# Both Gram products of the first macro step in one group, its v scaled by VectorE, and second-layer residuals on VectorE

## The chip, the cores and the metric

The kernel runs on one core of a Trainium2 chip. The metric is the device time of one execution in microseconds, from start to end of the program on that core; the median of several runs counts. TensorE is the matmul engine (PE in the profile; PEld are its weight loads), VectorE is DVE, ScalarE is ACT, GpSimd is POOL, and SyncE (SP) issues the DMAs here. TensorE's clock has two levels, 1.2 and 2.4 GHz; the granted clock in the profile is the mean as a share of the full one.

## The reference

A delta-rule attention over 768 steps (4 batches, 8 heads, head size 48) gives 3072 tokens of 384 values, which go through two dense layers pairs:

```
for t in range(S):                                  # S = 768
    y[t]  = q[t] @ state
    v_old = kn[t] @ state                           # kn: k over its norm
    state = state + beta[t] * outer(kn[t], v[t] - v_old)
h   = x @ w_in                                      # 384 -> 1024
s   = h * softmax(h)
ln  = (s - mean(s)) / sqrt(var(s) + 1e-6) * g_ln
x2  = ln @ w_out                                    # 1024 -> 384
h2  = x2 @ w_in2                                    # 384 -> 2048
out = (h2 * sigmoid(1.702 * h2)) @ w_out2           # 2048 -> 384
```

The weights arrive as 64-bit floats.

## The kernel before

**Tiling.** The sequence is cut into 24 blocks of 32 steps; four blocks make a macro step, and there are six macro steps. For a macro step m the kernel computes for each of its blocks n the Gram products k.k and k.q (`gram(n)`), solves the triangular systems of all four blocks at once on VectorE (`solve(m)`, which writes the factors `dt` by way of DRAM), and then goes through the blocks in order (`recur(n)`): correction of v with the state, matrix of factors, output y, update of the state `mv`. `layer1(n, y)` does the first dense layer, softmax and normalisation of the block's 128 tokens and transposes the result; `layer1_out(g)` (tags B0 to B5) multiplies by `w_out` for 512 tokens, and `layer2(g)` (C0 to C5) does the second pair of layers for these. All large products are made of three fp16 products of high and low parts.

**Weights.** `weights()` converts 42 blocks: 6 of w1, 8 of wo1, 12 of w2 and 16 of wo2, in this order by layer, the last two mixed. A block is loaded (L476), turned from 64-bit to fp32 by ScalarE and VectorE (L479 to L491), rounded to fp16 on ScalarE (L504), and the rounding's residual becomes the low part. There are two ways for the residual. Up to block number `PRM["pe"]` (38.322) TensorE does it: an fp32 matmul with a scaled unit matrix (L510) and an fp16 matmul with a negative one (L511) leave the residual in PSUM, and ScalarE copies it out (L513). From there on (blocks 39 to 42) one VectorE instruction does it (L516).

**Gram products.** `gram(n)` loads k and q of the block (L560, L561), and `quads` issues 32 small fp32 matmuls (8 heads by 4 batches; the profile counts 64 for them, with as many weight loads) of a block into one PSUM bank. In the first macro step (m == 0) these are two groups: k.k with 32 columns (L577), and k.q with 32 columns (L594), with priority `late`. VectorE masks k.k (L586), writes it once more through another mask (L589, `below`), and masks k.q (L595). k.k is stored to DRAM (L597), and when all four blocks are there, the solve loads them (L606). In the later macro steps one group of 64 columns makes both.

**Scaling.** `recur(n)` multiplies v by a factor of `dt` on GpSimd (L736), before the first matmul of the block.

**Order.** Nothing in this kernel is ordered by hand. Every step is a task (`P.add`) with an engine, an assumed duration, what it reads and writes, and a priority. A planner (`Plan.emit`) goes through an assumed time and picks on each engine, among the tasks that could start first, the one with the lowest priority; the engines' programs are written in this order, DMAs in SP's. To a task's priority two tables add an offset: `OFF[tag]` and `OFF["tag|engine"]`, where the tag is that of the function's call (`gram0`, `w2_0_512`, `rec0`, `A0`, `B0`, ...). Where the planner sees TensorE pause before the first use of bank 0, it puts in filler matmuls on zeros (`busy`, recorded at L351).

Of the kernel before, what the change touches and what calls it, by code (L numbers as in the profile page):

```python
# [16 lines left out]
CH = 32  # L17
# [17 lines left out]
PRM = dict(bl=161.965, vm=-0.684, vo=-1.262, pe=38.322, near=22.976, al=0.0, af=0.658, xp=25.764, lp=1.945, go1=24.87, so1=49.904, ew=48, nx=6.743, kp=13.711, need=100.793, fg=0.161, f1=7.669, f3=1796.849, sp=0.084, gp=0.667, gq=99, cold=25.151, cf=-1.14, nb4=9.499, v1b=1.424, cut=0.473, el=22.0, la=0.602, d0=-55.31, d1=-18.518, d2=6.18, d3=1.2, a0=14.438, wo1s=1.606, nk=15.164, nb2=1.269, nb3=7.307, early=21.447, v1=-9.577, wa=0.829, U=36.161, T0=31.882, g0=0.697, a=-0.318, b=0.937, ao=18.661, go=231.282, gs=-2.989, so=-0.04, ss=0.661, w1=-840.745, wo1=-7.28, w2o=-52.255, w2s=8.446, wo2o=41.493, wo2s=4.056, nb=1.319, bs=0.333, cs=4.152, su=8.832, ld=47.69)  # L35
# [217 lines left out]
def kernel(  # L253
# [18 lines left out]
    PE, DVE, ACT, POOL, SP = nc.tensor, nc.vector, nc.scalar, nc.gpsimd, nc.sync  # L272
# [26 lines left out]
    w1 = [T("w1h", [128, K0, F1], FP16), T("w1l", [128, K0, F1], FP16)]  # L299
    wo1 = [T("wo1h", [128, K1, DM], FP16), T("wo1l", [128, K1, DM], FP16)]  # L300
# [44 lines left out]
    P = Plan()  # L345
# [7 lines left out]
    U, T0 = PRM["U"], PRM["T0"]  # L353
# [23 lines left out]
    def dve(n, f=1.0):  # L377
        return 0.145 + f * n / 960.0
# [4 lines left out]
    def pool(n):  # L383
        return 0.06 + n * 0.00207
# [155 lines left out]
    def quads(eng_fn, dur, r, w, prio, work=0.32):  # L540

        def mm():
            for h in range(H):
                for b in range(B):
                    eng_fn(h, b)
        P.add("PE", dur, mm, r=r, w=w, prio=prio, small=True, work=work)

    def gram(n):
        P.tag = f"gram{n}"
        m, s = divmod(n, SUB)  # L550
        base = due(SUB * m) - PRM["go1" if m == 1 else "go"] + PRM["gs"] * s if m else -1000.0 + s
        i, src = n % NKQ, kq[n]
        kb, lend = kqb[i], []
        if NKQ <= n < NKQ + 2:
            i, kb = f"l{n}", lnt[n - NKQ].bitcast(FP32).rearrange("p k t -> p (k t)")[:, 0:2 * H * 2 * CH].rearrange(
                "p (e h c) -> p e h c", e=2, h=H)
            lend = [f"lent{'hl'[n - NKQ]}{j}" for j in range(4)]

        def load():
            SP.dma_start(out=kb[64:64 + D], in_=src[0])  # L560
            SP.dma_start(out=kb[0:D], in_=src[1])  # L561
        P.add("SP", 2 * ISSUE, load, w=[f"kq{i}"] + lend, prio=base - 40, lat=2.2, nb=(0.0, max(base - 25, PRM["nb3"]), max(base - 25, PRM["nb4"]))[min(m, 2)])
        bk = Bank(SIDE)

        def product(c, w):
            def mm(h, b):
                r0, _ = cls(b)
                PE.matmul(bank(bk)[32 * b:32 * b + 32, 64 * h + c:64 * h + c + w], lhsT=kb[r0:r0 + D, b % 2, h, 0:CH],  # L568
                          rhs=kb[r0:r0 + D, b % 2, h, c:c + w], start=True, stop=True, tile_position=(r0, 32 * b))
            return mm  # L570
        gi = n % 2
        g_, p_, gp = gsb[gi], psb[gi], [f"gsb{gi}", f"psb{gi}"]
        if 2 <= n < 4:
            both = thb[n - 2].rearrange("p (a h c) -> p a h c", a=2, h=H)
            g_, p_, gp = both[:, 0], both[:, 1], [f"thg{n - 2}", f"th{n - 2}"]
        if m == 0:
            quads(product(0, CH), 0.6, [f"kq{i}"] + lend, [bk, gp[0]], base)  # L577
        else:
            quads(product(0, 2 * CH), 0.99, [f"kq{i}"] + lend, [bk] + gp, base, 0.37)
        mk = mask.unsqueeze(1).to_broadcast([128, H, 2 * CH])  # L580

        def ev(dst, c):
            return lambda: DVE.tensor_tensor(
                out=dst, in0=bank(bk).rearrange("p (h c) -> p h c", h=H)[:, :, c:c + CH],
                in1=mk[:, :, c:c + CH], op=ALU.mult)
        P.add("DVE", dve(256), ev(g_, 0), r=[bk, "mask"], w=[gp[0]], prio=base)  # L586
        late = base
        if m == 0:
            P.add("DVE", dve(256), lambda: DVE.tensor_tensor(  # L589
                out=below[s], in0=bank(bk).rearrange("p (h c) -> p h c", h=H)[:, :, 0:CH],  # L590
                in1=cross.unsqueeze(1).to_broadcast([128, H, CH]), op=ALU.mult),
                r=[bk, "cross"], w=[belowk[s], f"below{s}"], prio=base + PRM["bl"])
            late = -700.0 + n
            quads(product(CH, CH), 0.6, [f"kq{i}"] + lend, [bk, gp[1]], late)  # L594
        P.add("DVE", dve(256), ev(p_, CH), r=[bk, "mask"], w=[gp[1]], prio=late)  # L595
        gd = g_dr[m % 2][32 * s:32 * s + 32].rearrange("(h b) i j -> (b i) h j", b=B)
        P.add("SP", ISSUE, lambda: SP.dma_start(out=gd, in_=g_), r=[gp[0]], w=[f"gdr{m % 2}_{s}"],  # L597
              prio=base - 5, lat=dma(131072, 2))
        P.add("SP", ISSUE, lambda: SP.dma_start(out=p_dr[n % NPD], in_=p_), r=[gp[1]],
              w=[f"pdr{n % NPD}"], prio=late - 5, lat=dma(131072))  # L600
# [80 lines left out]
    def recur(n):  # L681
# [3 lines left out]
        m, s = divmod(n, SUB)  # L685
        base = due(n)
        md = m % 2
# [36 lines left out]
        def load_q():  # L724
            SP.dma_start(out=st[64:64 + D, 0:2], in_=qt[n, 0])
            SP.dma_start(out=st[0:D, 2:4], in_=qt[n, 1])
        P.add("SP", 2 * ISSUE, load_q, w=[f"stq{ist}"], prio=base - 20, lat=0.6, nb=base + 10 - PRM["ld"])

        def load_p():
            for b in range(B):  # L730
                w0 = cls(b)[1]
                SP.dma_start(out=st[w0:w0 + CH, b], in_=p_dr[n % NPD][32 * b:32 * b + 32])
        P.add("SP", 4 * ISSUE, load_p, r=[f"pdr{n % NPD}"], w=[f"stp{ist}"], prio=base - 20, lat=0.35, nb=base + 10 - PRM["ld"])

        dst, dk = (r_, f"r{ir}") if n == 0 else (v_, f"vt{iv}")
        P.add("POOL", pool(384), lambda: POOL.tensor_tensor(  # L736
            out=dst, in0=v_, in1=dt[:, s, :, CH:CH + 1].to_broadcast([128, H, D]), op=ALU.mult),
            r=[f"dt{md}_{s}", f"vt{iv}"], w=[dk], prio=base - 5)

        mvs = [f"mvs{c}" for c in range(4)]  # L740
        b1, b2, b3, b4 = Bank(SIDE), Bank(SIDE), Bank(SIDE), [Bank(SIDE), Bank(SIDE)]

        def hd(b):
            return bank(b)[:, 0:H * D].rearrange("p (h c) -> p h c", h=H)

        def ks(h, b):
            r0 = cls(b)[0]
            PE.matmul(hd(b1)[32 * b:32 * b + 32, h, :], lhsT=kr[r0:r0 + D, b % 2, h, :],
# [342 lines left out]
```

## Time and profile before

| | before |
|---|---|
| median of 3 runs | 839.51 us |
| runs | 835.08, 839.51, 845.69 us |
| profiled execution | 836.79 us |
| its span | 835.1 us |
| mean granted TensorE clock | 0.969 |
| TensorE, VectorE, ScalarE, GpSimd busy | 777.1, 589.5, 373.1, 247.2 us |

The span is from the first to the last instruction of the profiled execution; 1.7 us of its time lie outside. Durations below come from that execution. Busy time of TensorE contains fillers, and its records overlap, so the start of the next one is the better measure of what a matmul occupies.

### The profile page before, as it was taken

What the parts mean: (1) busy time and instruction counts of PE and PEld (TensorE: products, weight loads), DVE (VectorE), ACT (ScalarE), POOL (GpSimd) and SP (SyncE); (2) the same over time, 40 slices, a digit from 0 to 9 for tenths busy, and PEclk for the clock granted to TensorE, in tenths of its full rate; (3) what the DMA queues carried; (4) which work ended last, traced back from release to release, by engine and by line L of the source; (5) the groups of instructions that cost most, each with busy time, mean ns of one, the idle gap of its engine ahead of it and who ended that gap; (6) DMA issues with size and microseconds to landing.
All of it is one profiled execution on the core that took longest, in us unless ns stands there. A gap on an engine that the chain in (4) does not pass through costs nothing.

```text
span 835.1 us, 25208 instructions
## 1 busy us (share of the span) xinstructions
PE 777.1 (93%) x10642; PEld 389.7 (47%) x10642; DVE 589.5 (71%) x1456; ACT 373.1 (45%) x661; POOL 247.2 (30%) x240
## 2 busy tenths in 40 slices
PE   6568978999989999998999999999999999999997
PEld 4135554444555444544544444444444444444443
DVE  2896777999999999999999899964566445212111
ACT  0467564544326524544633545525554355422332
POOL 3020011110413354325531434504442222420322
PEclk7778898999999999999999999999999999999999
DMA  6898597976646466677736654365433252100101
GB/s 168 235 278 232 148 220 137 235 196 168 125 94 139 86 149 171 147 177 159 168 79 187 142 119 104 84 152 144 103 79 94 80 115 44 26 1 0 39 1 38
DMA packets 177314, 105.76 MB, mean 127 GB/s; under 512 B 128273, under 2 KB 161169, under 8 KB 177201
## 3 DMA queue, kind: packets, MB, share of 16 engines
q1 hardware_dynamic: 177200, 104.15, 52.7%
q8 instruction: 83, 1.36, 0.7%
q14 instruction: 31, 0.25, 0.1%
HBM read 66.16 MB, written 20.64 MB: 104 GB/s over the span
## 4 chain that ended last, share of the span: by engine, by line
PE 53%; DVE 27%; issue 9%; DMA 4%; ACT 3%; POOL 2%; POOLq 0%; SPq 0%; ACTq 0%; DVEq 0%
PE psum L1008 13%; PE psum L981 13%; PE psum L946 9%; PE psum L874 6%; DVE mv L836 4%; DVE trip L645 4%; DVE trt L642 4%; PE psum L568 3%; DVE th L989 2%; PE psum L351 2%; DVE mv L786 2%; DVE col L881 2%; PE psum L510 2%; ACT mv L782 2%; DVE eb L893 2%
## 5 line engine op out<-in xcount | busy, mean ns | idle before, releaser
L995 POOL TENSOR_TENSOR gl<-th,gh 128x512 f16<-128x512 f32 x90 | 107.3, 1192 | 236.0 <-ACT gh L992 167.8
L989 DVE SCALAR_TENSOR_TENSOR th<-th,psum 128x512 f32<-128x512 f32 x96 | 65.5, 683 | 89.0 <-ACT th L986 88.4
L1008 PE MATMUL psum<-gl,wo2h 128*128 128x512 f16 x288 | 109.1, 379 | 1.0 <-POOL gl L995 1.0
L1008 PE MATMUL psum<-gh,wo2h 128*128 128x512 f16 x288 | 109.5, 380 | 0.2 <-ACT gh L992 0.2
L981 PE MATMUL psum<-x2th,w2h 128*128 128x512 f16 x288 | 109.5, 380 | 0.1
L981 PE MATMUL psum<-x2th,w2l 128*128 128x512 f16 x288 | 109.1, 379 | 0.0
L981 PE MATMUL psum<-x2tl,w2h 128*128 128x512 f16 x288 | 109.1, 379 | 0.0
L1008 PE MATMUL psum<-gh,wo2l 128*128 128x512 f16 x288 | 109.1, 379 | 0.0
L986 ACT ACTIVATE th<-psum 128x512 f32<-128x512 f32 x96 | 56.9, 593 | 98.4 <-PE psum L981 93.6
L874 PE MATMUL psum<-w1h,xt 128*128 128x512 f16 x288 | 94.2, 382 | 1.5 <-DVE mv L836 0.8
L992 ACT ACTIVATE gh<-th 128x512 f16<-128x512 f32 x96 | 60.2, 627 | 68.9 <-DVE th L989 64.6
L1008 PEld LDWEIGHTS <-wo2h 128*128 128x128 f16 x576 | 56.2, 98 | 67.9 <-issue 2.1
L981 PEld LDWEIGHTS <-w2h 128*128 128x128 f16 x576 | 53.5, 98 | 62.0 <-issue 0.3
L642 DVE TENSOR_TENSOR trt<-trip 128x30 f32<-128x30 f32 (+9 forms) x150 | 71.3, 476 | 2.7
L645 DVE TENSOR_TENSOR trip<-trip,trt 128x30 f32<-128x30 f32 (+9 forms) x150 | 69.6, 464 | 2.4
L923 POOL TENSOR_TENSOR lnr<-eb,lnr 128x1024 f16<-128x1024 f32 x24 | 52.2, 2173 | 52.0 <-ACT lnr L921 52.0
L874 PEld LDWEIGHTS <-xt 128*128 128x128 f16 x432 | 40.0, 98 | 49.9 <-issue 2.5
L890 ACT ACTIVATE eb<-psum,col 128x512 f32<-128x512 f32 x48 | 36.9, 773 | 52.4 <-DVE col L886 52.1
L946 PE MATMUL psum<-lnth,wo1h 128*128 128x512 f16 x144 | 54.6, 379 | 0.4 <-DVE th L989 0.4
L874 PE MATMUL psum<-w1l,xt 128*128 128x512 f16 x144 | 54.8, 381 | 0.0
L946 PE MATMUL psum<-lnth,wo1l 128*128 128x512 f16 x144 | 54.6, 379 | 0.0
L946 PE MATMUL psum<-lntl,wo1h 128*128 128x512 f16 x144 | 54.6, 379 | 0.0
(210 smaller groups left out, 1246.6 us busy)
## 6 DMA issues: line engine op xcount, KB each, us to landing
kq<-kq SPq DMA_DIRECT2D x44, 192.0 KB, 4.4
stg<-w_in SPq DMA_DIRECT2D x11, 512.0 KB, 5.6
vt<-vt SPq DMA_DIRECT2D x24, 192.0 KB, 2.7
st<-qt SPq DMA_DIRECT2D x48, 96.0 KB, 2.9
kt<-kdr SPq DMA_DIRECT2D x48, 96.0 KB, 2.3
stg<-udr SPq DMA_DIRECT2D x48, 96.0 KB, 2.3
out<-ob SPq DMA_DIRECT2D x18, 256.0 KB, 2.7
ktr<-kd SPq DMA_DIRECT2D x46, 96.0 KB, 2.9
```

The lines of the kernel that those rows point to most:

```text
L642: DVE.tensor_tensor(out=tv, in0=tri[:, lo:hi, j:j + 1].to_broadcast([128, nr, j]), in1=tri[:, j:j + 1, 0:j].to_broadcast([128, nr, j]), op ...
L645: DVE.tensor_tensor(out=tri[:, lo:hi, 0:j], in0=tri[:, lo:hi, 0:j], in1=tv, op=ALU.add)
L874: PE.matmul(bank(bh[j]), lhsT=x[:, k], rhs=w_[:, k, 512 * j:512 * j + 512], start=(k == 0 and i == 0), stop=(k == K0 - 1 and i == 2))
L890: P.add("ACT", act(512) + 0.34, lambda j=j, ev=ev: ACT.activation(out=ev, in_=bank(bh[j]), func=ACTF.Exp, bias=cl(3), scale=cl(0), accum_o ...
L923: P.add("POOL", pool(F1), lambda: POOL.tensor_tensor(out=lnr[1], in0=e_, in1=lnr[0], op=ALU.subtract), r=["lnrh"] + [f"eb{ie}_{j}" for j i ...
L946: PE.matmul(bank(ba)[:, 0:w_], lhsT=wo1[a][:, k, oc], rhs=lnt[b][:, k, tk], start=(k == 0 and i == 0), stop=(k == K1 - 1 and i == 2))
L981: PE.matmul(bank(bh)[:, 0:w_], lhsT=w2[a][:, k, fc], rhs=x2t[b][:, k, tk], start=(k == 0 and j == 0), stop=(k == K0 - 1 and j == 2))
L986: P.add("ACT", act(w_), lambda: ACT.activation(out=th, in_=bank(bh)[:, 0:w_], func=ACTF.Tanh, scale=0.851 / (X2S * W2S)), r=[bh], w=[f"th{ ...
L989: P.add("DVE", dve(w_), lambda: DVE.scalar_tensor_tensor(out=th, in0=th, scalar=1.0, in1=bank(bh)[:, 0:w_], op0=ALU.add, op1=ALU.mult), r= ...
L992: P.add("ACT", act(w_), lambda: ACT.activation(out=gh, in_=th, func=ACTF.Copy), r=[f"th{i}"], w=[f"gh{i}"], prio=base)
L995: P.add("POOL", pool(w_), lambda: POOL.tensor_tensor(out=gl, in0=th, in1=gh, op=ALU.subtract), r=[f"th{i}", f"gh{i}"], w=[f"gl{i}"], prio= ...
L1008: PE.matmul(bank(acc[o])[:, 0:w_], lhsT=wo2[a][:, f, oc], rhs=gb[i][b][:, 0:w_], start=(f == 0 and j == 0), stop=(f == K2 - 1 and j == 2))
```

## The change

Three edits, and new tables.

- In the first macro step, too, one group of 64 columns makes both Gram products of a block. The separate group for k.q is gone.
- In the blocks of the first macro step v is scaled by VectorE instead of GpSimd.
- `PRM["pe"]` becomes 14: the 6 blocks of w1 and 8 of wo1 keep TensorE's way for the residual, and all blocks of w2 and wo2 take VectorE's.
- The table `OFF` has other numbers in all its entries, so the order on all queues can be another one. (Entries of engines that a task no longer uses are gone, as `w2_0_0|PE` and `rec0|POOL`.) No other parameter is changed.

```diff
-PRM = dict(bl=161.965, vm=-0.684, vo=-1.262, pe=38.322, near=22.976, ...)
+PRM = dict(bl=161.965, vm=-0.684, vo=-1.262, pe=14, near=22.976, ...)
...
-        if m == 0:
-            quads(product(0, CH), 0.6, [f"kq{i}"] + lend, [bk, gp[0]], base)
-        else:
-            quads(product(0, 2 * CH), 0.99, [f"kq{i}"] + lend, [bk] + gp, base, 0.37)
+        quads(product(0, 2 * CH), 0.99, [f"kq{i}"] + lend, [bk] + gp, base, 0.37)
...
             late = -700.0 + n
-            quads(product(CH, CH), 0.6, [f"kq{i}"] + lend, [bk, gp[1]], late)
         P.add("DVE", dve(256), ev(p_, CH), r=[bk, "mask"], w=[gp[1]], prio=late)
...
-        P.add("POOL", pool(384), lambda: POOL.tensor_tensor(
+        eng, cost, E_ = ("DVE", dve(384), DVE) if m == 0 else ("POOL", pool(384), POOL)
+        P.add(eng, cost, lambda: E_.tensor_tensor(
             out=dst, in0=v_, in1=dt[:, s, :, CH:CH + 1].to_broadcast([128, H, D]), op=ALU.mult),
-            r=[f"dt{md}_{s}", f"vt{iv}"], w=[dk], prio=base - 5)
+            r=[f"dt{md}_{s}", f"vt{iv}"], w=[dk], prio=base - 5, port=True)
```

## Rows read from the trace of the kernel before

**Rows 1.** The page, first part: busy time, share of the span, instructions.
```profile
PE 777.1 (93%) x10642; PEld 389.7 (47%) x10642; DVE 589.5 (71%) x1456; ACT 373.1 (45%) x661; POOL 247.2 (30%) x240
```

**Rows 2.** Busy time by stretch, all engines; then granted clock, DMA share, GB/s.
```profile
60.00:143.00 83.00, 69.31 (x1839) 43.21 (x1840) 59.22 (x142) 47.73 (x95) 10.33 (x8) 0.88 0.81 187
143.00:176.00 33.00, 31.96 (x508) 16.89 (x503) 30.04 (x95) 16.66 (x29) 5.52 (x4) 1.00 1.04 214
176.00:200.00 24.00, 24.00 (x226) 11.53 (x225) 23.59 (x66) 10.33 (x19) 0.00 (x0) 1.00 0.63 176
200.00:540.00 340.00, 327.35 (x4862) 164.89 (x4860) 317.92 (x779) 155.86 (x272) 133.90 (x120) 1.00 0.60 137
540.00:700.00 160.00, 158.53 (x2033) 77.06 (x2032) 92.85 (x219) 72.96 (x130) 51.07 (x48) 1.00 0.42 101
700.00:835.10 135.10, 129.17 (x597) 58.22 (x595) 26.10 (x48) 46.11 (x76) 37.05 (x31) 1.00 0.09 21
```

**Rows 3.** The chain that ended last, 6 to 26 us: start, us, what.
```profile
11.00 1.26 issue
...
15.31 2.32 issue
...
19.52 0.42 DVE th L583
19.94 0.34 DVE dt L589
...
20.69 2.87 issue
...
25.00 5.80 DMA trip<-gdr
```

**Rows 4.** DMA issues, 0 to 200 us: count, KB each, median us to landing.
```profile
gdr<-gsb SPq DMA_DIRECT2D x13, 128.0 KB, 4.0
...
lnth<-kq SPq DMA_DIRECT2D x2, 192.0 KB, 3.9
```

**Rows 5.** The timeline, SP and TensorE, first 160 us: start, us, engine, line.
```profile
9.08 0.43 SPq L561 DMA_DIRECT2D lnth<-kq  x1
...
13.00 1.08 PE L568 MATMUL psum<-kq 48*32 48x32 f32 x63
...
154.68 1.10 PE L568 MATMUL psum<-kq 48*32 48x64 f32 x64
```

**Rows 6.** Line 736 alone: ns shortest/median/longest, first and last start.
```profile
L736 POOL TENSOR_TENSOR vt<-vt,dt x23: 837/843/1286, 61.5 to 661.8; 128x384 f32<-128x384 f32 x23
...
L736 POOL TENSOR_TENSOR rb<-vt,dt x1: 3347/3347/3347, 58.2 to 58.2; 128x384 f32<-128x384 f32 x1
```

**Rows 7.** The chain that ended last, 0 to 200 us, further pieces.
```profile
58.22 3.36 POOL rb L736
...
66.12 0.94 PE psum L510 x2
...
131.56 0.22 PE psum L511
...
187.12 0.86 PE psum L510 x2
```

**Rows 8.** Groups by line and shape: busy us, mean ns of one, idle before.
```profile
L752 DVE TENSOR_TENSOR rb<-vt,psum 128x384 f32<-128x384 f32 x23 | 12.5, 545 | 6.6 <-PE psum L748 6.5
...
L483 DVE SCALAR_TENSOR_TENSOR fst<-fst,stg 128x512 int32<-128x512 int32 x7 | 4.8, 686 | 0.2
...
L483 DVE SCALAR_TENSOR_TENSOR fst<-fst,stg 128x384 int32<-128x384 int32 x6 | 3.3, 552 | 0.0
```

**Rows 9.** Line 511 alone, 60 to 143 us: ns, first and last start.
```profile
L511 PE MATMUL psum<-wo2h,neg x8: 326/326/326, 66.9 to 119.7; 128*128 128x384 f16 x8
L511 PE MATMUL psum<-w2h,neg x8: 379/379/634, 67.9 to 141.9; 128*128 128x512 f16 x8
```

**Rows 10.** Line 351 (fillers) by stretch: PE, PEld, granted clock, DMA share, GB/s.
```profile
143.00:176.00 33.00, 16.08 (x69) 6.43 (x69) 1.00 1.04 214
```

More of the change, by code (lines that the diff above doesn't have):

```diff
@@ new lines @@
+PRM = dict(bl=161.965, vm=-0.684, vo=-1.262, pe=14, near=22.976, al=0.0, af=0.658, xp=25.764, lp=1.945, go1=24.87, so1=49.904, ew=48, nx=6.743, kp=13.711, need=100.793, fg=0.161, f1=7.669, f3=1796.849, sp=0.084, gp=0.667, gq=99, cold=25.151, cf=-1.14, nb4=9.499, v1b=1.424, cut=0.473, el=22.0, la=0.602, d0=-55.31, d1=-18.518, d2=6.18, d3=1.2, a0=14.438, wo1s=1.606, nk=15.164, nb2=1.269, nb3=7.307, early=21.447, v1=-9.577, wa=0.829, U=36.161, T0=31.882, g0=0.697, a=-0.318, b=0.937, ao=18.661, go=231.282, gs=-2.989, so=-0.04, ss=0.661, w1=-840.745, wo1=-7.28, w2o=-52.255, w2s=8.446, wo2o=41.493, wo2s=4.056, nb=1.319, bs=0.333, cs=4.152, su=8.832, ld=47.69)
```

3 lines of the change are left out of this document (1 added, 2 removed).

## The prediction

> **What bounds the kernel now.** I first read the page's shares of busy time: TensorE is busy 93% of the span [rows 1], so the question is where its other 7% lies and how much of its work is not needed. The view of busy time in stretches answers that [rows 2]. From 200 us to the end TensorE idles 12.7, 1.5 and 5.9 us in three stretches that add up to 635 us: there the time is the matmuls themselves, and only fewer matmuls can shorten it. VectorE is at 94% from 200 to 540 us, but at 58% in the next stretch, so work added to it there is caught up long before the end. Up to 200 us the picture is another one. From 60 to 143 us TensorE idles 13.7 of 83 us at a mean granted clock of 0.88, and from 143 to 176 us it looks full only because 16.1 of its 33 us are filler matmuls on zeros [rows 10]. So the first 176 us, up to the first output product of layer 1, are a chain of waits (Gram products, solve, four recurrences, four softmaxes), and the change works nearly wholly in them. I then read the chain that ended last in that part, and priced each piece of the change from it.
>
> **Both Gram products in one group.** Today each of the four blocks' sequences of small matmuls stands twice, with 32 columns each, so that k.k leaves early and k.q follows. The chain shows what that costs. A second product starts only when VectorE has read the first out of the bank, twice (0.42 and 0.34 us), and part way through a second product TensorE stands still, three times, for 1.26, 2.32 and 2.87 us, waiting for nothing that the profile shows [rows 3]. The stops come at every second group of 64 matmuls, so I take them for something that counts instructions, their fetch; that is inferred. The last k.k leaves VectorE at some 20.3 us, and the load of all Gram blocks for the solve is issued at 25.00 us, after the last k.q product and its stop [rows 3]. In one group, half of the instructions go, and with them some two of the stops. What is late then is the last of the four input loads: its second half is issued at 9.08 us [rows 5] and lands 3.9 us after that [rows 4], at 13.0 us. A group of 64 columns takes 1.10 us later on, and one of 32 columns took 1.08 us here [rows 5], so I estimate 1.7 us. With one stop of 2.3 us and the eviction of 0.42 us the last block leaves at 17.4 us, its store lands 4.0 us later [rows 4], and the solve's load can be issued at 21.4 us: 3.6 us earlier. The bounds are 6 us (no stop at all) and 0 (the input loads move back on SP by as much, behind the weight loads that share its queue). A loss is excluded as long as SP's order puts these loads no later, since the group itself is shorter than the two that it replaces.
>
> The rows show a stop at every second group. The Trainium skill ("Runtime: NRT & Kernel Launch", Instruction fetch mechanics) says that crossing into the next block of instructions is "mostly hidden". By that rule no stop would go with the instructions, only the wait for VectorE ahead of the second products would, and the total would be 2 us worse; the trace, whose stops have no other releaser, speaks for the 3.6 us.
>
> **v scaled by VectorE.** The first scaling waits on GpSimd for the solve's factors and then takes 3.35 us, against a median of 0.84 us for the other 23 [rows 6]; it stands alone on the chain from 58.22 to 61.58 us [rows 7]. Why it is four times as long, no row tells. A VectorE operation of that size takes 0.55 us [rows 8], so 2.8 us go; the lower bound is 0.3 us (0.84 less 0.55), if this one was only unlucky. What is new is that the wait for the factors now stands in VectorE's queue: the weight conversions behind it wait too, and through them ScalarE's rounding. If the order puts it one conversion too early or too late, that is 0.55 to 0.69 us [rows 8]. The other three scalings add 1.6 us to VectorE, of which I count half, 0.8 us, as on the path; GpSimd had them free.
>
> **Second-layer residuals on VectorE.** 24 of the 38 weight blocks (twelve of w2, twelve of wo2) lose two fp32 passes, one fp16 matmul and one ScalarE copy each, and gain one VectorE operation. 16 of them lie from 60 to 143 us [rows 9], six from 143 to 176 us and two after that. The two after it lie in the TensorE-bound part and take 1.08 us each (0.86 [rows 7] and 0.22): 2.2 us go outright. The six lie among fillers, which take their place: nothing. Of the 16, seven stand on the chain, in 14 pieces from 66.12 to 131.78 us that add up to 9.4 us [rows 7]; the others lie beside it. In return VectorE gets one operation of 0.55 us for a block of 384 columns and of 0.69 us for one of 512, the price of its conversions of these shapes [rows 8]: 16 times 0.62 is 9.9 us in that stretch. VectorE is 71% busy there [rows 2], so part of it falls into its pauses and part delays the chain, which itself runs over VectorE in places. I take half, 5.0 us: net 4.4 us gained. The ends are 9.4 us gained (all hidden) and 0.5 us lost (none hidden).
>
> **The order.** Every task's offset is new, on all queues; which instruction then stands before which can't be read from the diff. After 200 us an order can gain at most the idle time that is left, 20 us [rows 2], most of which are short waits, and it can lose as much. I take zero, and 6 us either way in the range.
>
> **The sum.** 3.6, and 2.8 less 0.8, and 4.4 and 2.2 us make 12.2 us. The profiled execution took 836.79 us, so it would take 824.6 us. The median of the three runs before is 839.51 us, 2.7 us above it; the median counts, so the forecast is 827 us, 1.5% faster. A measurement of this kernel can tell about 2% from no change (its own runs spread over 1.3%), so the likeliest outcome is "within 2%".
>
> **The rivals.**
> First, more is gained. The 16.1 us of fillers before the first output product of layer 1 are waiting time of the fourth softmax and its transposes [rows 10]. If the new order lets that chain run with less between its steps, half of them go (8 us), and all of the 9.4 us with them (5 us more than counted): 814 us. For it: TensorE has room there. Against it: VectorE is 91% busy from 143 to 176 us and the DMA engines have none at all (share 1.04) [rows 2]. Chance 0.22.
>
> Second, the chain gives it back. An earlier start of the solve meets the same weight loads and conversions, and the recurrences wait for DMA and not for TensorE; then only the 2.2 us of the TensorE-bound part remain: 837 us. For it: the DMA share is 0.81 and 1.04 in the two stretches [rows 2]. Chance 0.21.
>
> Third, slower: VectorE becomes the bound of the first 176 us. It gets 22 residuals at 0.62 us and four scalings at 0.55 us there, 15.8 us. If all of that is on the path, and the saved TensorE time is only pauses, the head grows by 15.8 us and 2.2 us come back after it: 853 us. The point at which it decides is VectorE's busy share from 60 to 143 us: 59.2 us of 83 now [rows 2], about 71 of 83 after, which is 86% and not yet full. It would have to pass some 95%. Chance 0.07.
>
> Fourth, the clock. With some 15 us less of matmuls from 60 to 143 us (16 blocks at 1.08 us or three quarters of it), TensorE's granted clock there may fall from its mean of 0.88 [rows 2], between the two levels of 1.2 and 2.4 GHz, to some 0.7. The work that remains, about 52 us, would take 13 us more, half of it on the path: 834 us. Against it: the kernel puts in fillers where its plan sees a pause, and the clock stays at 1.00 where they run [rows 2, 10]. Chance 0.05. The Trainium skill ("TensorE: Matmul & The Clock Gate", Part 1) puts it as "the default state is throttled, and activity releases the throttle", which speaks against taking work off TensorE; the two stretches, at 0.88 with pauses and at 1.00 without, agree.
>
> That the change doesn't do what it says is hardly possible for the three edits, whose instructions are fixed by the code.
>
> **How the numbers follow.** The forecast's case has 0.45. Its own terms move it by some 8 us either way (the Gram groups between 0 and 6, the residuals between 9.4 and -0.5, the order by 6). The range reaches from 808 us, below the first rival, to 846 us, above the second and fourth, and leaves the third and the tails out. Faster by over 2% means under 822.7 us: a fifth of the forecast's case and nearly all of the first rival, 0.30. Slower by over 2% means above 856.3 us: the upper part of the third rival, 0.04. The rest, 0.66, is within 2%.
>
> **What would show it.** The load of the Gram blocks is issued near 21 us and no longer at 25 us, with one or two stops of TensorE before it. The first scaling is a VectorE operation near 0.55 us, and the first recurrence starts some 6 us earlier than at 61.6 us. TensorE has 14 residual blocks, none of them of the second layer. The first output product of layer 1 starts near 166 us instead of 176 us; from there to the end it takes as long as now less 2 us. I am wrong if that start is where it was with VectorE busy above 95% before it (third rival), if it is there with VectorE's pauses as now (second), or if the part behind it has changed by more than 6 us, which would be the order.

## The result and the profile after

The changed kernel takes 851.77 us, the kernel before 839.52 us, medians of 20 runs each. The ratio is 1.0144 with a 95% interval from 1.0119 to 1.0169: 12 us slower, where 12 us faster was predicted. It is within 2% of before, as the prediction held likeliest, but on the other side of the forecast and above its range (808 to 846 us). Two of the changed kernel's 20 runs took 909.75 and 1128.85 us at a lower granted clock, and the ratio leaves them out.

The profiled execution took 852.37 us (span 850.7, mean granted clock 0.967). Its page's first part, and its stretches (start and end; length; busy time of TensorE, its weight loads, VectorE, ScalarE, GpSimd, each with its count; granted clock, DMA share, GB/s), to hold against [rows 1, 2]:

```profile
PE 787.4 (93%) x10437; PEld 390.0 (46%) x10437; DVE 596.0 (70%) x1484; ACT 362.9 (43%) x637; POOL 245.1 (29%) x236
```
```profile
60.00:143.00 83.00, 69.33 (x1749) 42.45 (x1749) 55.13 (x148) 32.59 (x61) 5.94 (x4) 0.88 0.75 172
143.00:176.00 33.00, 31.55 (x380) 15.83 (x379) 31.31 (x92) 16.60 (x29) 7.64 (x4) 1.00 0.64 163
176.00:200.00 24.00, 22.60 (x224) 10.86 (x223) 21.64 (x55) 8.23 (x16) 1.35 (x1) 1.00 0.47 127
200.00:540.00 340.00, 322.27 (x4788) 161.96 (x4787) 311.35 (x763) 153.05 (x268) 128.89 (x115) 0.99 0.59 141
```

TensorE has 205 matmul records fewer and is busy 10 us longer, because it has 123 fillers more. VectorE, which got 24 residuals and four scalings, is busy 4.1 us less from 60 to 143 us than before, not 12 more: part of its work there comes later. The next rows are single lines of the same trace: SyncE's timeline (start, us) and TensorE's in the last Gram group, then groups by line with shortest/median/longest ns, first and last start: the first scaling, the fillers, and the output products of layer 1.

```profile
21.95 0.33 SPq L602 DMA_DIRECT2D trip<-gdr  x1
```
```profile
10.96 0.41 PE L568 MATMUL psum<-kq 48*32 48x64 f32 x10 [0.53 <-DMA kq<-kq]
12.53 1.05 PE L568 MATMUL psum<-kq 48*32 48x64 f32 x50 [1.16 <-issue]
```
```profile
L733 DVE TENSOR_TENSOR rb<-vt,dt x1: 537/537/537, 55.2 to 55.2; 128x384 f32<-128x384 f32 x1
```
```profile
L351 PE MATMUL psum<-zeros x251: 377/379/634, 1.1 to 178.5; 128*128 128x512 f16 x126
```
```profile
L943 PE MATMUL psum<-lnth,wo1h x144: 376/379/390, 178.7 to 778.6; 128*128 128x512 f16 x144
```

The first steps came as predicted. The solve's load is issued at 21.95 us (25.00 before [rows 3]), one stop of TensorE is left before it (1.16 us; one or two were predicted), the first scaling takes 0.54 us on VectorE (3.35 [rows 6]), and the first recurrence starts at 55.7 us instead of 61.6. Then the lead is lost: block 2's recurrence starts at 110.0 us (103.8 before), the first output product at 178.7 (175.9), and from there to the end it takes 672.0 us instead of 659.2. There are 251 fillers instead of 128. The granted clock doesn't tell the two kernels apart: 0.967 and 0.969 over the whole span.

### The profile page after: what moved, and what is told of

Its sections match the earlier page's. It is cut to its first block, busy times and chain, and to the rows that moved or that the text cites. A ratio compares the mean times of both kernels' runs of the same rounds, so it can differ in the third digit from the quotient of the medians.

```text
span 850.7 us, 24783 instructions
## 1 busy us (share of the span) xinstructions
PE 787.4 (93%) x10437; PEld 390.0 (46%) x10437; DVE 596.0 (70%) x1484; ACT 362.9 (43%) x637; POOL 245.1 (29%) x236
## 4 chain that ended last, share of the span: by engine, by line
PE 39%; DVE 31%; issue 3%; ACT 2%; DMA 2%; SPq 1%; POOL 1%; POOLq 0%; ACTq 0%; DVEq 0%
PE psum L978 13%; PE psum L1005 12%; PE psum L943 6%; PE psum L871 5%; DVE mv L833 4%; DVE trt L638 4%; DVE trip L641 3%; DVE th L986 2%; DVE mv L783 2%; DVE col L878 1%; DVE eb L890 1%; ACT mv L779 1%; PE psum L789 1%; DVE trip L629 1%; DVE rb L749 1%
## 5 line engine op out<-in xcount | busy, mean ns | idle before, releaser
L978 PEld LDWEIGHTS <-w2h 128*128 128x128 f16 x576 | 53.6, 98 | 62.3
L351 PE MATMUL psum<-zeros 128*128 128x512 f16 x251 | 66.1, 414 | 6.5 <-DVE zeros L350 6.5
L638 DVE TENSOR_TENSOR trt<-trip 128x30 f32<-128x30 f32 (+9 forms) x150 | 69.2, 461 | 2.2
L641 DVE TENSOR_TENSOR trip<-trip,trt 128x30 f32<-128x30 f32 (+9 forms) x150 | 67.3, 448 | 2.4
L920 POOL TENSOR_TENSOR lnr<-eb,lnr 128x1024 f16<-128x1024 f32 x24 | 55.7, 2320 | 41.4 <-ACT lnr L918 39.2
L908 POOL TENSOR_TENSOR col<-col,half 128x1 f32<-128x1 f32 x24 | 13.8, 575 | 175.4 <-DVE col L906 162.0
L943 PE MATMUL psum<-lntl,wo1h 128*128 128x512 f16 x144 | 54.6, 379 | 1.4 <-DMA lntl<-lnr 1.4
L871 PE MATMUL psum<-w1l,xt 128*128 128x512 f16 x144 | 55.1, 383 | 0.0
```

The source lines that it names most:

```text
L351: P.fill.append((gate, until, lambda: PE.matmul(psum[0], lhsT=z, rhs=z.unsqueeze(1).to_broadcast([128, 4, 128]), start=True, stop=True)))
L638: DVE.tensor_tensor(out=tv, in0=tri[:, lo:hi, j:j + 1].to_broadcast([128, nr, j]), in1=tri[:, j:j + 1, 0:j].to_broadcast([128, nr, j]), op ...
L641: DVE.tensor_tensor(out=tri[:, lo:hi, 0:j], in0=tri[:, lo:hi, 0:j], in1=tv, op=ALU.add)
L871: PE.matmul(bank(bh[j]), lhsT=x[:, k], rhs=w_[:, k, 512 * j:512 * j + 512], start=(k == 0 and i == 0), stop=(k == K0 - 1 and i == 2))
L920: P.add("POOL", pool(F1), lambda: POOL.tensor_tensor(out=lnr[1], in0=e_, in1=lnr[0], op=ALU.subtract), r=["lnrh"] + [f"eb{ie}_{j}" for j i ...
L943: PE.matmul(bank(ba)[:, 0:w_], lhsT=wo1[a][:, k, oc], rhs=lnt[b][:, k, tk], start=(k == 0 and i == 0), stop=(k == K1 - 1 and i == 2))
```

## The experiments

Three groups of runs. Medians are of 5 to 12 runs each beside the kernel before on the same chip (839.81 to 841.24 us); ratios are to it, with 95% intervals. A ratio isn't the quotient of the two medians and lies up to 0.2% from it (f_all, f_v), so small differences between runs are read from the ratios. The last four columns are each run's one profile, which can lie some us from its run's median (before 2.7 us under it, f_both 4.4 us above): granted clock from 60 to 143 us, and the start (us) of block 0's and block 2's recurrence and of the first output product.

| run | us | ratio | clock | rec 0 | rec 2 | output |
|---|---|---|---|---|---|---|
| before | 839.52 | 1 | 0.88 | 61.6 | 103.8 | 175.9 |
| changed | 851.77 | 1.0144 [1.0119, 1.0169] | 0.88 | 55.7 | 110.0 | 178.7 |
| f_gram | 834.0 | 0.9927 [0.9891, 0.9964] | 0.98 | 57.7 | 97.6 | 167.0 |
| f_v | 839.36 | 1.0014 [0.998, 1.0048] | 0.89 | 59.6 | 101.1 | 174.1 |
| f_gv | 838.43 | 0.9956 [0.9922, 0.999] | 0.94 | 54.5 | 98.1 | 169.1 |
| f_res | 841.18 | 1.0025 [0.9997, 1.0052] | 0.77 | 62.6 | 105.4 | 171.6 |
| f_both | 841.59 | 1.0007 [0.9974, 1.0039] | 0.90 | 62.1 | 106.4 | 176.6 |
| f_none | 840.03 | 0.9974 [0.9947, 1.0001] | 0.71 | 62.3 | 104.5 | 173.1 |
| f_all | 836.73 | 0.9983 [0.9951, 1.0016] | 0.75 | 53.2 | 98.6 | 165.8 |
| a_q | 851.46 | 1.0107 [1.0065, 1.0148] | 0.88 | 54.6 | 109.0 | 174.1 |
| f_hm | 843.47 | 1.0038 [1.0008, 1.0067] | 0.78 | 54.4 | 104.2 | 168.9 |
| h_fa | 842.73 | 1.001 [0.9978, 1.0043] | 0.71 | 55.6 | 101.1 | 170.5 |
| h_a2 | 852.52 | 1.0145 [1.01, 1.0189] | 0.84 | 55.2 | 114.3 | 179.7 |
| h_f2 | 857.76 | 1.0204 [1.0177, 1.0231] | 0.76 | 54.2 | 114.8 | 180.5 |
| h_w | 872.39 | 1.0382 [1.0346, 1.0418] | 0.85 | 62.8 | 114.2 | 196.7 |
| h_w2 | 872.33 | 1.0391 [1.0357, 1.0425] | 0.80 | 54.1 | 110.8 | 192.7 |
| r_off | 864.09 | 1.0274 [1.0228, 1.0321] | 0.94 | 61.3 | 109.9 | 194.2 |
| r_offb | 851.53 | 1.0141 [1.0108, 1.0174] | 0.79 | 52.9 | 94.1 | 181.8 |
| r_pert | 854.51 | 1.0163 [1.0123, 1.0202] | 0.94 | 63.2 | 105.2 | 172.9 |
| r_gram | 837.17 | 0.9957 [0.9923, 0.9991] | 0.84 | 57.2 | 99.0 | 172.1 |

### The edits, in the order of before

Here the planner goes on seeing the tasks of before, with their engines and durations; only what a task emits is another instruction. So the order is held, and an edit is seen without a new plan. Two theories stood at the start: the new order cost the time (1), or the work added to VectorE's queue did (2).

**f_gram**: one Gram group, at the first group's place.
```diff
-            quads(product(0, CH), 0.6, [f"kq{i}"] + lend, [bk, gp[0]], base)
+            quads(product(0, 2 * CH), 0.6, [f"kq{i}"] + lend, [bk, gp[0]], base)
...
-            quads(product(CH, CH), 0.6, [f"kq{i}"] + lend, [bk, gp[1]], late)
+            quads(lambda h, b: None, 0.6, [f"kq{i}"] + lend, [bk, gp[1]], late)
```


> The kernel before with the first edit alone: one group of 64 columns per block of the first macro step makes both Gram products, at the place of the first group; every other instruction of every engine stays where it was in the order of before. Theory 1 (the new order on the queues cost the time, the three edits themselves gain): the solve's load leaves SP near 22 us instead of 25, the recurrence starts some 3 us earlier, and 3 us or a little less reach the end: 836 us beside 839.5. Theory 2 (the edits that load VectorE's queue cost the time): says the same of this kernel, since VectorE gets nothing here. Were it slower than before, the group itself would be at fault.

It gained 0.73%, 6 us. Its chain up to the solve (start, us, what), against [rows 3]:
```profile
13.76 1.11 PE psum L568 x60
14.87 0.02 issue
14.89 0.42 DVE th L583
15.32 0.03 DVE dt L589
15.35 7.14 DMA gdr<-th
22.49 0.02 issue
...
22.55 4.85 DMA trip<-gdr
```
The stops of 1.3 to 2.9 us are gone, all of them; in their place the last store takes 7.14 us (4.0 was the median before [rows 4]). The load is issued at 22.55 us, 2.5 us earlier than before.

Where the stops stand tells more than their number. Counted with the fillers, the three of before come ahead of TensorE's 224th, 352nd and 480th matmul, 128 apart; the one in the changed kernel comes ahead of the 224th, with 64 columns instead of 32. In f_gram TensorE had waited for the input load nine matmuls ahead of that place, and there is no stop:
```profile
13.00 0.30 PE L568 MATMUL psum<-lnth 48*32 48x64 f32 x4 [1.76 <-DMA lnth<-kq]
```
So a stop goes with a count of instructions, and f_gram's missing one may only be covered by that wait.

**f_v**: `POOL.tensor_tensor(...)` becomes `(DVE if m == 0 else POOL).tensor_tensor(...)`, at the same place. **f_gv**: f_gram and f_v together.

> The kernel before with the second edit alone: the four scalings of v in the first macro step run on VectorE, each at the place in the order where GpSimd's stood; no other instruction moves. Theory 1 (order): the first takes 0.55 us instead of 3.35, so 2 to 3 us are gained: 837 us beside 839.5. Theory 2 (VectorE's queue): the scalings wait in VectorE's queue for the solve's factors and for the loads of v, the weight conversions behind them wait as well, and the time comes out at 842 to 846 us.

> The two edits of the first macro step alone, one Gram group and the scaling of v on VectorE, in the order of before; the residuals stay on TensorE. Alone the first gave 0.73%, the second nothing. If the two lie one behind the other on the chain into the first recurrence, as predicted, that starts near 54 us and the time is 831 to 834 us; if the second only moves a wait, 834 to 836 us.

The scaling alone moved the first recurrence by 2.0 us and the end by nothing that can be measured. With the Gram group it starts 3 us earlier than with that alone, and the end is no earlier: 838.43 us, above both ranges expected of f_gv. Theory 2's loss isn't there either.

**f_res**: VectorE's residual where ScalarE's copy stood, for the blocks after the 14th; TensorE's two products are left out.
```diff
-            P.add("ACT", act(n), lambda: ACT.activation(out=dl, in_=bank(bk)[:, 0:n], func=ACTF.Copy),
-                  r=[bk], ...
+            P.add("ACT", act(n), (lambda: DVE.scalar_tensor_tensor(out=dl, in0=fv, scalar=sc, in1=dh,
+                  op0=ALU.mult, op1=ALU.subtract)) if late else lambda: ACT.activation(...),
+                  r=[bk] + (fk + [wk + "h"] if late else []), ...
```
**f_both**: the same, but TensorE's products stay, unread. **f_none**: TensorE's products are left out and VectorE gets nothing; ScalarE's copy stays as `ACT.activation(out=dl, in_=fv, func=ACTF.Copy, scale=0.0)`.

> The kernel before with the third edit alone: the residuals of the 24 second-layer weight blocks that TensorE made are made by VectorE, each at the place in the order where ScalarE's copy stood; TensorE's passes for them are left out and not replaced. Theory 1 (order): 4.4 us in the first 176 us and 2.2 us behind it are gained, 833 us beside 839.5. Theory 2 (VectorE's queue): 15 us more work on VectorE before 176 us delay the recurrences and softmaxes, 845 to 850 us.

> As the third edit alone (residuals of 24 second-layer blocks on VectorE, 841.2 us), but TensorE's passes for these blocks stay in as well, with nobody reading their result. That run lost 1.7 us against before though TensorE had some 24 us less to do, and its granted clock from 60 to 143 us was 0.77 against 0.88. Theory A (TensorE's passes stood in pauses and held the clock up, so leaving them out gains nothing): here the clock is back at 0.88 or above, the matmuls of the four recurrences are as short as in before, and the time is 841 us or less. Theory B (leaving them out gained the predicted 6 us, and VectorE's added operations cost 8): here only the cost is left, 846 to 849 us.

> TensorE's passes for the residuals of the 24 second-layer blocks are left out, and VectorE gets nothing in their place: ScalarE's copy stays and writes zeros as the low part, so the second layer is computed without the low parts of these weights. This is the gain of taking work off TensorE by itself. Theory A (pauses and clock): at most 2 to 3 us, 836 to 840 us, with a granted clock below 0.88 from 60 to 143 us. Theory B: the predicted 6.6 us or more, 831 to 833 us.

The stretch from 60 to 143 us, one row each of f_gram, f_res, f_both and f_none (columns as above):
```profile
60.00:143.00 83.00, 70.11 (x1936) 42.35 (x1931) 65.13 (x173) 50.58 (x99) 8.02 (x7) 0.98 0.83 193
```
```profile
60.00:143.00 83.00, 59.52 (x1832) 40.96 (x1836) 69.01 (x160) 42.33 (x82) 11.34 (x8) 0.77 0.82 189
```
```profile
60.00:143.00 83.00, 68.72 (x1844) 42.59 (x1846) 66.11 (x158) 41.28 (x79) 10.98 (x8) 0.90 0.84 187
```
```profile
60.00:143.00 83.00, 63.40 (x1772) 42.85 (x1774) 61.07 (x143) 47.87 (x94) 11.14 (x8) 0.71 0.82 188
```
And the recurrence's products of the same step (ns, first and last start), of before and of f_none:
```profile
L765 PE MATMUL psum<-rb,dt x256: 198/248/284, 61.6 to 128.5; 32*32 32x48 f32 x128
```
```profile
L765 PE MATMUL psum<-rb,dt x256: 201/276/283, 62.3 to 129.1; 32*32 32x48 f32 x128
```
Without TensorE's passes the granted clock falls, from 0.88 before [rows 2] to 0.71, and the recurrence's own matmuls get longer, from a median of 248 to one of 276 ns. That isn't one profile's chance: over the whole span the clock is 0.947 to 0.959 in the twelve executions of f_none and 0.961 or more in 28 of the 29 of before beside them (0.957 in the other). f_none, which only takes work away, gains 0.26% (2.2 us, interval from 4.5 us gained to nothing). Theory A held; how much of the missing gain is the clock and how much the pauses in which the passes stood, these runs don't separate. f_res itself lies between the numbers of theories 1 and 2. With the passes kept (f_both), VectorE's operations cost 0.6 us, interval 2.2 us gained to 3.3 us lost; without them (f_res against f_none) 0.51%, 4.3 us, though the two intervals just touch. One place where f_res pays is the chain to the second layer; its view of TensorE's waits from 171 to 200 us:
```profile
PE psum L981 <- DVE x2tl L953: 3.7, 1, 3.7
```
The first product of layer 2 waits 3.7 us for an eviction that stands in VectorE's queue behind the second layer's weights.

**f_all**: the three edits at once. 

> The kernel before with all three edits, in the order of before: nothing but the changed instructions is in another place. It differs from the changed kernel in its order alone. Theory 1 (order): the predicted gain of about 12 us, or most of it, shows here: 827 to 833 us. Theory 2 (VectorE's queue): as slow as the changed kernel, 848 to 854 us.

836.73 us, between the two theories' numbers and much nearer to the first: theory 2 fell, and so did the predicted gain. The first output product starts at 165.8 us, where the prediction put it (166), but nine of these ten us are given back behind it (668.3 us to the end of its span, 834.1, instead of 659.2). TensorE is busy there for 639.2 us, as before (639.1), so the nine us are waits, 3.6 of them the wait for the second layer's first product that f_res has too. VectorE's busy time from 60 to 143 us is 70.9 us, as predicted (71), at a clock of 0.75:
```profile
60.00:143.00 83.00, 59.91 (x1762) 39.81 (x1753) 70.87 (x179) 40.18 (x76) 5.66 (x4) 0.75 0.76 180
```
f_all differs from the changed kernel in its order and in what the planner makes with it, the fillers (128 against 251) and the choice of PSUM banks. So **the order, with these, costs 1.0144 less 0.9983, 1.6% or some 13 us (15 by the medians), and the edits are worth 0.2% (interval 0.5% gained to 0.2% lost)**.

The two traces also tell where. Behind the first output product TensorE idles 29.0 us in the changed kernel and 29.1 in f_all; the changed kernel's 3.7 us more there are TensorE's work (643.0 us against 639.2). What the order costs is lost ahead of that product.

### The order, piece by piece

These runs have the changed kernel's tasks. The planner's result is collected, rearranged, and then emitted, in all of them but a_q with the PSUM banks given out anew:
```diff
-            t.fn()
+            self.out.append(t)
...
+    for i in ORDER:
+        tasks[i].fn()
```
"Old" is f_all's order, "new" the changed kernel's own. VectorE's waits from the first recurrence to the first output product (what waited, for what: us, times, longest), of the changed kernel and of f_all:
```profile
DVE col L853 <- PE psum L789: 6.5, 2, 3.3
DVE rb L773 <- PE psum L767: 5.2, 3, 3.7
DVE rb L749 <- PE psum L745: 3.8, 2, 3.6
DVE mv L783 <- ACT mv L779: 3.1, 4, 1.9
DVE wo2h L481 <- DMA wo2h<-w_out: 2.8, 1, 2.8
```
```profile
DVE mv L786 <- PE psum L757: 3.4, 2, 2.2
DVE rb L776 <- PE psum L770: 2.5, 2, 2.1
DVE wo2l L481 <- DMA wo2l<-w_out: 2.0, 1, 2.0
```
All such rows add up to 27.7 us in the new order and 12.1 us in the old. An instruction of VectorE's queue that waits holds up those behind it, and in the new order such waits are 15.6 us longer. The sum alone doesn't rank orders, though: from the same places of their traces it is 23.8 us in before and 23.1 in r_gram, which lose nothing.

**a_q** repairs the plainest place, by moving three tasks ahead of others: block 2's load of v (470) ahead of its loads of k, its scaling (473) and subtraction (475) ahead of a weight conversion. In the changed kernel block 2's subtraction (`rb`, L749) stood behind a weight load and its own v. On VectorE (start, us):
```profile
105.90 0.37 DVE L481 TENSOR_SCALAR wo2h<-wo2h 128x384 int32<-128x384 int32 x1 [2.81 <-DMA wo2h<-w_out]
...
107.90 0.56 DVE L733 TENSOR_TENSOR vt<-vt,dt 128x384 f32<-128x384 f32 x1 [0.57 <-DMA vt<-vt]
...
109.44 0.55 DVE L749 TENSOR_TENSOR rb<-vt,psum 128x384 f32<-128x384 f32 x1
```
```diff
+MOVES = [(470, 469), (473, 166), (475, 166)]
```


> The changed kernel in its own order, with three instructions moved: block 2's load of v goes on SyncE's queue ahead of the four loads of k for that block (93 us instead of 103.8), and its scaling and the subtraction behind it go in VectorE's queue ahead of the weight conversions whose loads are late (after the mask of gram 7 instead of after the wait at 105.9 us). Theory 1 (order; in the new order block 2's recurrence waits behind loads that others wait for in VectorE's queue): the first matmul of block 2's recurrence at 102 us instead of 110.0, and most of these 8 us reach the end: 844 to 846 us instead of 851.8. If the chain of the head is bound elsewhere, 850 us or more, with block 3 as late as now.

The subtraction now ran at 100.63 us, and yet block 2's recurrence started at 109.0. TensorE and VectorE in a_q:
```profile
100.63 0.55 DVE L749 TENSOR_TENSOR rb<-vt,psum 128x384 f32<-128x384 f32 x1 [1.69 <-PE psum L745]
```
```profile
102.66 0.38 PE L871 MATMUL psum<-w1h,xt 128*128 128x512 f16 x1
...
107.35 1.67 PE L351 MATMUL psum<-zeros 128*128 128x512 f16 x7
108.96 0.88 PE L762 MATMUL psum<-rb,dt 32*32 32x48 f32 x64
```
Block 1's first-layer products and seven fillers stood ahead of it on TensorE; the fillers alone are 1.6 us in which its operand was ready. The expectation of 844 to 846 us was missed; against the changed kernel the intervals overlap. **f_hm** puts this one feature into the old order: block 1's six first-layer tasks and their two reductions ahead of block 2's subtraction.

> The three edits in the order of before (836.7 us), with one feature of the new order put in: block 1's 18 first-layer matmuls and their two reductions stand ahead of block 2's recurrence on TensorE and VectorE. Moving block 2's scaling and subtraction ahead in the changed kernel brought its recurrence only from 110.0 to 109.0 us, because these matmuls and seven fillers stood ahead of it on TensorE all the same. If giving the softmax of block 1 precedence over the recurrence of block 2 is what the head loses by, the recurrence's first matmul moves from 98.6 to 103 us or later, and 4 to 6 us reach the end: 840 to 843 us. If the two only change places without a loss, 836 to 838 us.

It cost 0.55% against f_all, 4.6 us, as expected (the two intervals just overlap): precedence of a softmax over the recurrence is likely one part of the loss. No run emits the old order unchanged by this route, with its banks given out anew, so a share of the 4.6 us may be the route's. **h_fa** (old order up to the first output product, new behind it), **h_a2** (new up to block 2's first product with the state, old behind it) and **h_f2** (old up to there, new behind it) look for the stretch:
```
head = first[:first.index(cut)]
ORDER = head + [i for i in second if i not in head]
```


> The changed kernel's instructions in two orders: up to the first output product of layer 1 in that of the kernel before (with the three edits, as in the run that took 836.7 us), and from there in the changed kernel's own. It tells which stretch of the new order costs the 15 us. By the two traces the head takes 12.9 us longer in the new order and the rest 3.7 us: if the head costs it, 838 to 841 us; if the later order costs it and the head's delay would have been caught up anyway, 848 us or more.

> The changed kernel's instructions in its own order up to block 2's first product with the state (some 95 us), and from there in the order of before. It bounds where the head loses: by the traces, before that point the new order costs 1 to 4 us, and between it and block 2's recurrence 8 us. If the loss comes from what follows 95 us (block 1's first layer and softmax ahead of block 2's recurrence, and the later order), the first output product starts near 168 us and the time is 837 to 840 us. If the loss was already laid down before (weight blocks that the new order converts later, Gram products of the next macro step that it makes earlier), the first output product starts at 173 us or later and the time is 843 us or more.

> The changed kernel's instructions in the order of before up to block 2's first product with the state (some 95 us), and from there in the new order: the converse of the run of 852.5 us. If the loss is laid down before 95 us, this comes out like the run with the old head up to the first output product, 841 to 845 us. If what follows 95 us costs it as well (the softmax of block 1 ahead of block 2's recurrence cost 4.6 us when put into the old order), 846 to 850 us.

h_fa puts 1.3% (1.0144 less 1.001, 11 us) on the new head, and 0.3% on the order behind it, which is within the intervals. But these runs don't cut the head further: h_a2 is as slow as the new order, and h_f2 is slower still, beyond both ranges expected of it. In h_a2 block 2's recurrence starts at 114.3 us, later than in either whole order, because the tasks that the old order would have done by then come first. **h_w** (new order, weight tasks of the head at the old order's places, counted from the recurrences' TensorE steps) and **h_w2** (the converse) exchange one kind of task:

> The changed kernel in its own order, but up to the first output product the tasks of the weight blocks (loads, conversions, residuals, on all queues) stand where they stand in the order of before, counted from the recurrences' TensorE steps. Theory 3 (the new order leaves too few weight conversions between the recurrences' steps, so that VectorE waits for TensorE with nothing to do, 27.7 us against 12.1, and makes them up later on the chain): VectorE's waits fall below 20 us, the first output product starts at 168 to 172 us instead of 178.7, and the time is 841 to 846 us. Theory 4 (the rest of the head's order costs it: softmax of block 1, Gram products and solve of the next macro step ahead of the recurrences): 849 us or more.

> The converse: the three edits in the order of before (836.7 us), but up to the first output product the tasks of the weight blocks stand where the new order has them, counted from the recurrences' TensorE steps. Theory 3: VectorE waits longer than 20 us and the time is 845 to 850 us. Theory 4: 836 to 840 us.

Both miss both theories: +3.8% and +3.9%, far slower than either order whole. The places of the weights and of the rest can't be exchanged one without the other, so these two runs don't tell which of them is at fault.

### Orders planned anew

**r_off**: the code of before with the changed kernel's table `OFF`. **r_offb**: the changed code with the table of before. **r_pert**: no edit; the planner assumes 1 ns more for each VectorE operation. **r_gram**: the first edit as the change has it, the second group's task gone, so that the plan is new.
```diff
-        return 0.145 + f * n / 960.0
+        return 0.146 + f * n / 960.0
```


> The kernel before with nothing changed but the table of offsets, which is that of the changed kernel; the planner makes a new order from it. If the offsets cost the time by themselves (an order that gives the first stretch's chain less precedence), 848 us or more; if they only fit badly together with the edits, 842 us or less. As the planner's order answers to every duration, it isn't the very order of the changed kernel.

> The changed kernel with the old table of offsets; the planner makes the order anew, for the new instructions and their durations. With the old code and the old table 839.5 us, with the old code and the new table 864, with the new code and the new table 851.8, this is the fourth corner. If the offsets decide: 834 to 842 us. If the planner's order breaks down as soon as the instructions change under a table that was made for others (as the old code with the new table did): 848 us or more.

> The kernel before with no edit at all, except that the planner assumes 1 ns more for each VectorE operation; code, table and instructions are those of before, only the order is planned anew. If the order of before is one lucky point of its table and a new plan loses 1 to 3% by itself, 848 us or more. If plans from the same table are about equally good, 836 to 844 us, and the loss belongs to this case's new order.

> The kernel before with the first edit alone (one Gram group of 64 columns; 834.0 us in the order of before), written as in the change, so that the planner makes a new order from the old table. If a new plan loses by itself, 845 us or more; if the edit decides, 832 to 837 us.

r_pert has every instruction (but 197 fillers instead of 128) and every offset of before and is 1.6% slower, as much as the changed kernel. It loses elsewhere: its first output product,
```profile
L946 PE MATMUL psum<-lnth,wo1h x144: 377/379/389, 172.9 to 782.9; 128*128 128x512 f16 x144
```
starts 3 us earlier than before, but from there to the end of its span of 854.6 us it takes 681.7 us instead of 659.2: 59 of its 197 fillers, 13.0 us, stand there (two before), and TensorE idles 27.6 us instead of 20.1. r_offb, with the table that was good for the old code, is as slow as the changed kernel with its own. r_off is worse than both. r_gram came out at 837 us, so a new plan doesn't always lose. Five new plans, the changed kernel's among them, stand at -0.4, +1.4, +1.4, +1.6 and +2.7% to before.

## Why the prediction was wrong

**The step that failed is "The order", "I take zero, and 6 us either way".** It measured some 13 us lost, by f_all against the changed kernel; without it the three edits alone, at 836.7 us, would have been in the range. Two things were wrong with the zero. The prediction looked for the order's worth only after 200 us, and the loss lies ahead of that: h_fa puts 11 us on the head, and behind the first output product TensorE idles as long in the new order as in the old (29.0 and 29.1 us). And as much to gain as to lose is the middle of what is possible, not of what plans here give: the mean of the five above is +1.4%, 11 us, and r_pert lost 1.6% with no instruction changed but the number of fillers.

**The other terms** were to give 12.2 us together and gave 0.2% (interval 0.5% gained to 0.2% lost). The third rival had the right sign and, with 853 us, nearly the measured time, but by luck: its mechanism is absent, since VectorE's busy time from 60 to 143 us fell to 55.1 of 83 us, far from its 95%.

**Both Gram products in one group**: right in mechanism. 3.6 us were predicted, with bounds of 0 and 6; the run alone gave 6 us (interval 3.0 to 9.2). Two or three stops went with the halved number of instructions, and their places bear out that they go with a count. The last block left VectorE at 15.3 us instead of the predicted 17.4, its store took 7.14 us instead of 4.0, and so the load left SyncE 2.5 us earlier, not 3.6. The rest was gained between the solve and the first output product, where the one profile has a higher clock; why isn't settled. The Trainium skill's "mostly hidden" ("Runtime: NRT & Kernel Launch", Instruction fetch mechanics) fits f_gram, where TensorE had waited 1.76 us just ahead of the place and no stop shows. It doesn't fit before and the changed kernel, where the waits ahead of the places were shorter (0.85, 0.87 and 0.87 us, and 0.53) and TensorE stood still for 1.26, 2.32 and 2.87 us, and for 1.16.

**v scaled by VectorE**: the 3.35 us operation went, as said, and the first recurrence came 2.0 us earlier; but the 2.0 us net didn't arrive at the end (interval 1.7 us gained to 4.0 lost). It stood in the chain of that stretch; what bounded the rest of the head instead, no run shows.

**Second-layer residuals**: both terms were mis-sized. Leaving out TensorE's passes was to give 9.4 and 2.2 us; f_none gives 2.2 in all. The fourth rival, with a chance of 0.05, had named a reason: the clock. In the six runs with the passes left out and no more than 128 fillers (f_res, f_none, f_all, f_hm, h_fa, h_w2) the clock from 60 to 143 us is 0.71 to 0.80; in the eight with the passes, in any order, 0.84 to 0.98. The six kernels without the passes and with more fillers, 164 to 251, are at 0.76 to 0.88 and overlap both; the changed kernel is at 0.88 with 251. VectorE's added operations were to cost 5.0 us and cost 0.6 to 4.3. Against the 2.2 us of two blocks in the TensorE-bound part stands a wait of 3.7 us of the second layer's first product for VectorE (f_res).

In the order of before the edits come out at 836.7 us. That is the second rival's number (837) by chance: in it the head doesn't get earlier, and here it does, by ten microseconds, nine of which are given back later.

**What stays open**: which features of the new head make up its 11 us. Precedence of block 1's softmax is worth up to 4.6 of them when put into the old order, and VectorE waits 15.6 us longer; no cut or exchange isolated the rest. No run has the new order without its 123 additional fillers either, so what they cost or give isn't shown; their number doesn't rank the runs (h_w2, with 128, is among the slowest). The best kernel of these runs is f_gram, 0.7% faster than before: the first edit in the order of before.

## What to carry to other kernels

When a change comes with a new schedule, price the schedule as a change of its own, from how far other schedules of the same work lie apart; hold the order and exchange the instruction, and both parts can be measured. Matmuls that stand in TensorE's pauses needn't be a cost that can be taken out: here taking out 24 blocks' passes gave 2.2 us, and the granted clock fell. And on an in-order queue ask of every operation that is moved onto it what stands behind it while it waits.

## What the runs showed of the hardware

The clock from 60 to 143 us fell from 0.88 to 0.71 when nothing but two passes and one matmul per weight block were left out (f_none), and the recurrence's matmuls of 32x48 from a median of 248 to one of 276 ns. A stop of TensorE of 1 to 3 us comes ahead of its 224th matmul in before and in the changed kernel alike, and in before again 128 and 256 matmuls later. GpSimd's first scaling isn't slow by chance: it took 3.35, 3.40 and 3.29 us in three kernels of one order (before, f_gram, f_res) and 3.39 and 4.30 us in two other orders (r_pert, r_off), with 0.84 us as the median of the others before [rows 6]. In before VectorE runs instruction upon instruction beside it, and the one that is under way when the scaling ends, at 61.6 us, is longer as well, 1.22 us instead of 0.69 for its shape:
```profile
60.18 0.69 DVE L483 SCALAR_TENSOR_TENSOR w2l<-w2l,stg 128x512 int32<-128x512 int32 x1
60.91 1.22 DVE L491 SCALAR_TENSOR_TENSOR w2l<-stg,w2l 128x512 int32<-128x512 int32 x1
```
That the two engines keep each other waiting there is inferred. A store of a Gram block, 4.0 us in the median before [rows 4], took 7.14 us on the chain of f_gram.
